# Second-half weights at set times, one store for each quad, and squares one step sooner in a fused attention and gated-MLP kernel

## The chip, the cores and the metric

The kernel runs on one core of one Trainium2 chip. The metric is the device time of that core in microseconds (us). A profile is one execution of the program under the hardware profiler. Its span is about 1.8 us shorter than the time of the same execution. The engines are called TensorE (PE in the profile), VectorE (DVE), ScalarE (ACT), GpSimd (POOL) and SyncE (SP, which issues the DMAs; SPq is its queue).

## The reference, cut to what matters

```python
def reference(A_x, A_wqkv, A_wo, B_x, B_w_in, B_w_sp, B_b_sp, B_w_out, gate_w):
    def _A_ref(x, wqkv, wo):          # S = 2048, D = 1024, H = 32 heads of 32
        ...                           # each position sees 8 keys at distances 0, 2, ..., 14
        logits = jnp.einsum('bhsd,bhswd->bhsw', q, kg) * scale
        attn = _softmax(logits, axis=-1)
        o = jnp.einsum('bhsw,bhswd->bhsd', attn, vg)
        return o.transpose(0, 2, 1, 3).reshape(B, S, D) @ wo

    def _B_ref(x, w_in, w_sp, b_sp, w_out):          # Fh = 1792
        z = _gelu(jnp.einsum('bsd,df->bsf', x, w_in))
        z1 = z[..., :Fh]
        z2 = _layernorm(z[..., Fh:], axis=-1)
        g = jnp.einsum('ts,bsf->btf', w_sp, z2) + b_sp[None, :, None]
        return jnp.einsum('bsf,fd->bsd', z1 * g, w_out)

    g = _sigmoid((x * gate_w).sum(-1, keepdims=True))
    return g * _A_ref(...) + (1 - g) * _B_ref(...)
```

## The kernel before

The kernel runs in stages: the projections of attention, then z2 (two halves of its columns, p = 0 with 7 quads and p = 1 with 8), then z1 (7 steps of two quads), then the spatial product with w_sp, then the two output products. Attention's own arithmetic is done by VectorE and runs alongside the projections and z2.

Every large product is done in "quads": a Strassen-like scheme with 7 products of half-size blocks on four PSUM banks. Two quads run interleaved as a pair, which is 56 matmuls: about 10.5 us for z2 (448 columns each) and 12 us for z1 (512 columns). Between the products of a quad come additions that VectorE makes from one PSUM bank into another (`plus`). TensorE cannot go on without them: the fifth product overwrites the bank Y that the first addition reads. What stands in VectorE's queue in front of such an addition can therefore stop TensorE.

```python
    def chain(A11, A12, A22, S1, S2, S3, S4, B11, ..., vs, put, share, N, ...):
        def plus(out, a):
            dve(N / 960.0 + 0.14, clock["PE"] + 0.2)
            last_add[0] = nc.vector.tensor_tensor(out[:, n], a[:, n], vs, ALU.add)   # L485
            return last_add[0]
        ...
        product(X, pairs(A11, B11), True, N)             # 1; product() is L424
        last_seed[0] = nc.scalar.copy(Y[:, n], X[:, n])
        yield
        product(V, pairs(S1, T1), True, N)               # 2
        with tc.high_priority():
            share(vs, V[:, n])                           # L503
        yield
        product(Y, pairs(S2, T2), False, N)              # 3
        with tc.high_priority():
            plus(Z, Y)                                   # first addition
        yield
        product(X, pairs(A12, B21), False, N)            # 4
        ...
        yield
        product(Y, pairs(S3, T3), False, N)              # 5
        ...
            inst = plus(V, Y)                            # second addition
        ...
        product(Z, pairs(S4, B22), False, N)             # 6
        ...
        product(W, pairs(A22, T4), False, N)             # 7
```

The weights of a quad also need four sums on VectorE (`sums4`, S1 to S4) before its second product. For p = 1 these are four sums of 128 x 1792, about 1.08 us each, and for each z1 step four sums of 0.42 us.

The order of instructions in the z2 stage is fixed while the program is built. A builder keeps a virtual clock for each engine (`clock`), collects loads (`due`) and small pieces of VectorE work (`fill`) with the time at which each may start, and puts an instruction into the program when the virtual clock comes to that time (`advance`). `act`, `dve` and `pe` book time on it. `settle` then pins the order on every engine. From z1 on, the framework's scheduler decides the order by itself.

```python
    def load_later(p, at, gap):           # z2 weights: 8 steps of 2 DMAs
        def landed(t):
            land[0] += 1
            if land[0] == KT:
                fill.extend((t, 1.05, f) for f in wz_sums(p))
        for n, f in enumerate(load_wz(p)):
            dma(at + gap * n, 0.65, f, landed)
    ...
    load_later(1, clock["PE"], 1.2)
    mark(banks[4:8], ZC)
    for n in range(0, len(quads), 2):     # z2: attention's VectorE work is filled in by step()
        ...
        run(*[z2_quad(*q) for q in quads[n:n + 2]], step=quad_step)
    drain()                               # the rest of attention
    settle()
    live[0] = False
    ...                                   # z1
    for fp in range(3):
        load_w1(fp)                       # two DMAs each
    w1_sums(0)
    mark(banks, 512, ZC)                  # one matmul of 64 columns on each bank
    for fp in range(NFH):
        if fp + 1 < NFH:
            w1_sums(fp + 1)
        for a in ((), (0,), (1, 2), (3, 4), (5, 6), (7,), ())[fp]:
            load_raw(0, a)                # transposing load of w_sp, behind the last z1 store
        run(z1_quad(fp, 0), z1_quad(fp, 1), hooks={2: lambda: between(fp)})   # between: squares
        ...                               # normalize(n) when four more rows have their squares
        if fp + 3 < NFH:
            load_w1(fp + 3)
```

`load_raw` writes a part of SBUF in which attention's buffers stood, so the first of these loads also waits for the last store of attention's output to DRAM (o_d).

Of the kernel before, what the change touches and what calls it, by code (L numbers as in the profile page):

```python
# [13 lines left out]
P = 128  # L14
# [11 lines left out]
FH = 1792  # L26
# [32 lines left out]
def kernel(  # L59
# [31 lines left out]
    z1_d = dpool.tile([4, P, NF * 512], BF, name="z1_d")  # L91
# [161 lines left out]
    def dma(ready, dur, f, landed=None):  # L253
        if not live[0]:
            return f()
        item = [ready, dur, f, landed]
        due.append(item)
        return item

    def issue(item):  # L260
        if item in due:
            due.remove(item)
            ready, dur, f, landed = item
            sp = take("SP", 0.62, max(ready, lanes[-8]))
            end = take("DMA", 1.2 * dur, sp + 0.6) + 1.1
            lanes.append(end)
            f()
            if landed is not None:
                landed(end)
# [148 lines left out]
    last_store = [None]  # L418
    wait_for = [None, None, None]
# [385 lines left out]
    def z2_quad(p, i, side=None):  # L805
        vs = vz_slots[(i + p) % 2]
        w, s = wz[p], wzs[p]

        share = nc.vector.tensor_copy if p else nc.scalar.copy
        return chain([w[0][:, k, :] for k in K4], [w[0][:, 4 + k, :] for k in K4], [w[1][:, 4 + k, :] for k in K4],  # L810
                     *[[s[q][:, k, :] for k in K4] for q in range(4)], *x_tiles(i), vs,
                     lambda m, a, bank: z2_gelu(p, i, m, a, bank), share, ZC, flip=True, side=side, lean=LEAN[p])

# [8 lines left out]
    def square(n, x, junk):  # L822
        c = slice(x * HF, (x + 1) * HF)
        return nc.scalar.activation(junk[:, c], z2[:, z2_row(n), c], ACT.Square, accum_out=(s2, s2h)[x][:, n:n + 1])  # L824
# [46 lines left out]
    def load_later(p, at, gap):  # L871
        land = [0.0]

        def landed(t):
            land[0] += 1
            if land[0] == KT:
                fill.extend((t, 1.05, f) for f in wz_sums(p))
        for n, f in enumerate(load_wz(p)):
            dma(at + gap * n, 0.65, f, landed)
# [32 lines left out]
    load_later(1, clock["PE"], 1.2)  # L912
    mark(banks[4:8], ZC)
    junk = reg(R_OFF + 12288, FH)
    SQ_AT = (2, 9)
    for n in range(0, len(quads), 2):
        p, i = quads[n]
        if p == 1 or quads[n + 1][0] == 1:
            t = clock["PE"]
            while fill or due:  # L920
                t += 0.25
                advance(t)
        count = [0]

        def quad_step():
            hold[0] = count[0] != 1
            step()
            count[0] += 1
            if p == 1 and (NG - 2, 1) in multiplied and count[0] in SQ_AT and squares[0][0] < 2 * i and len(squares) > 32 - SQH:
                act(0.9, clock["PE"])  # L930
                square(*squares.pop(0), junk)
        run(*[z2_quad(*q) for q in quads[n:n + 2]], step=quad_step)
    hold[0] = False
    drain()
    settle()
    live[0] = False
    pinned.clear()
# [40 lines left out]
    def load_raw(c, a):  # L978
        row = 4 * c + (a % 4) + 8 * (a // 4)
        inst = sync.dma_start_transpose(raw_slots[c][:, :, a, :], wsp_v[row])  # L980
        tc.add_manual_dep(inst.ins, last_store[0].ins.name, NOSYNC, reason="behind the stores")
# [19 lines left out]
    w1_slots = [free(R_OFF + o, 2048).rearrange("p (k f c) -> p k f c", k=KT, f=2) for o in (36864, 30720, 32768)]  # L1001
    ws_slots = [free(R_OFF + o, 2048, F16).rearrange("p (q k c) -> p q k c", q=4, k=4) for o in (38912, 34816)]
    z1s_slots = [free(T1_OFF + 2048 * r, 2048).rearrange("p (f a t) -> p f a t", f=2, a=2) for r in range(2)]
    zv_slots = [free(R_OFF + 20480 + 1024 * r, 1024, F32) for r in range(2)]

    def load_w1(fp):
        for f in range(2):
            sync.dma_start(w1_slots[fp % 3][:, :, f, :], win_v[:, :, HF * f + fp * P:HF * f + (fp + 1) * P])
# [5 lines left out]
    def z1_quad(fp, c):  # L1014
# [6 lines left out]
        def gelu(f, a, bank):  # L1021
            last_gelu[0] = nc.scalar.activation(z1s[:, f, a, :], bank[:], ACT.Gelu_apprx_tanh)  # L1022

        def store():
            for a in range(2):
                dst = z1_d[c + 2 * a].rearrange("p (f t) -> p f t", f=NF)[:, fp:fp + NFH + 1:NFH, :]
                last_store[0] = sync.dma_start(dst, z1s[:, :, a, :])
# [9 lines left out]
    def between(fp):  # L1037
        left = max(6 - fp, 1)
        for _ in range(-(-len(squares) // left)):
            sq = square(*squares.pop(0), z1_junk)  # L1040
            tc.add_manual_dep(sq.ins, last_seed[0].ins.name, NOSYNC, reason="behind the first copies of the quads")

    for fp in range(3):
        load_w1(fp)
    w1_sums(0)
    mark(banks, 512, ZC)
    for fp in range(NFH):
        if fp + 1 < NFH:
            w1_sums(fp + 1)
        for a in ((), (0,), (1, 2), (3, 4), (5, 6), (7,), ())[fp]:  # L1050
            load_raw(0, a)
        if fp == 6:
            wsp_sums(0, 0)
        run(z1_quad(fp, 0), z1_quad(fp, 1), hooks={2: lambda: between(fp)})
        while fp and ready[0] + 4 <= (squares[0][0] if squares else 16):
            n = ready[0]
            nc.vector.tensor_tensor(s2[:, n:n + 4], s2h[:, n:n + 4], s2[:, n:n + 4], ALU.add)
            normalize(n)
# [4 lines left out]
    def load_z1(n):  # L1063
        c, fp = divmod(n, NFH)
        for a in range(2):
            src = z1_d[c + 2 * a].rearrange("p (f t) -> p f t", f=NF)[:, fp:fp + NFH + 1:NFH, :]
            sync.dma_start(z1_slots[n % 2][:, :, a, :], src)
# [211 lines left out]
```

## Time and profile before

| before | |
|---|---|
| times | 680.09, 680.32, 680.32 us: median 680.32 us |
| the profiled execution | 683.96 us (span 682.2 us, mean granted clock 0.995) |
| TensorE busy | 97% of the span |

TensorE is the bound nearly everywhere. The page's first part gives each engine's busy time, share of the span and number of instructions. The clock row gives the granted TensorE clock in tenths of full speed (9 is 90% or more) for 40 slices of about 17 us:

```profile
PE 662.7 (97%) x4193; PEld 317.2 (47%) x4193; DVE 453.6 (66%) x671; ACT 294.3 (43%) x619; POOL 6.3 (1%) x15
...
PEclk9999999999998999999999999999999999999999
```

So the question is what lies in the remaining holes. As a measure, I summed over all pairs of successive matmuls the time from start to start, less columns/2.4 GHz. In this document "holes" means that sum over a stretch, worked out from the trace. A matmul of 448 columns that waits for nothing starts 0.187 us after the one before. From 197 to 380 us, the stretch that the change touches, the profiled execution has 15.9 us of such excess. The waits view says on what (line of the waiter and of what it waited for; us in total, number, longest):

```profile
PE psum_all L424 <- DVE psum_all L485: 8.6, 5, 4.8
```

The timeline of TensorE in the first half of z2, which runs from about 197 to 240 us (start, duration, the group, and in brackets the idle time before it and what ended it) shows two of them:

```profile
205.04 10.75 PE L424 MATMUL psum_all<-arena 128*128 128x448 f16 x56 [1.45 <-DVE psum_all L485]
220.62 5.73 PE L424 MATMUL psum_all<-arena 128*128 128x448 f16 x18 [4.83 <-DVE psum_all L485]
```

The timeline of VectorE says what stood in front of the two additions (L485): first four sums of the first z1 weights, of which the first is shown (128 x 512, each 0.42 us), and later three sums of the second z2 weights (128 x 1792), which themselves had waited 3.03 us for their load. These weights are for the second half, from about 240 us on; their sums only stood in front of additions of the first.

```profile
202.90 0.42 DVE L560 TENSOR_TENSOR arena<-arena 128x512 f16<-128x512 bf16 x1
...
204.36 0.62 DVE L485 TENSOR_TENSOR psum_all<-psum_all,arena 128x448 f32<-128x448 f32 x1
...
216.81 3.22 DVE L556 TENSOR_TENSOR arena<-arena 128x1792 f16<-128x1792 bf16 x3 [3.03 <-DMA arena<-in_B_w_in_dram]
219.94 1.16 DVE L485 TENSOR_TENSOR psum_all<-psum_all,arena 128x448 f32<-128x448 f32 x2
```

After the long hole the clock is halved for a while. The windows view (stretch, length, then busy time and instructions of PE, of its weight loads, of DVE, ACT and POOL, then the clock, the share of the DMA engines and GB/s) shows 12 matmuls in 4.28 us, against 0.187 us each at full clock:

```profile
218.00:224.90 6.90, 4.28 (x12) 1.72 (x12) 5.77 (x7) 1.75 (x6) 0.00 (x0) 0.52 0.02 8
```

The Trainium skill ("TensorE: Matmul & The Clock Gate", Part 1) names two states of the clock for a kernel like this one, full and half, and says that an idle window of about 3.4 us halves it. This trace agrees: after 4.83 us of idleness the clock is 0.50 for 6.83 us.

SyncE's queue: all loads and stores of this stage are issued by this one queue, in order. The "arena<-in_B_w_in_dram" at 191.38 and 193.16 are the two loads of the first z1 weights, which the scheduler has placed here on its own, among attention's band stores (band_d). The 16 others are the second z2 weights. att_L is attention's load of its last logits.

```profile
191.38 0.42 SPq L186 DMA_DIRECT2D arena<-in_B_w_in_dram  x1
191.85 1.26 SPq L186 DMA_DIRECT2D band_d<-arena  x2
193.16 0.64 SPq L186 DMA_DIRECT2D arena<-in_B_w_in_dram  x1
193.95 4.68 SPq L186 DMA_DIRECT2D band_d<-arena  x2
198.68 1.50 SPq L186 DMA_DIRECT2D arena<-in_B_w_in_dram  x2
200.28 1.25 SPq L186 DMA_DIRECT2D band_d<-arena  x2
201.58 3.96 SPq L186 DMA_DIRECT2D arena<-in_B_w_in_dram  x6
205.64 1.57 SPq L186 DMA_DIRECT2D att_L<-band_d  x2
207.27 5.71 SPq L186 DMA_DIRECT2D arena<-in_B_w_in_dram  x8
```

The Trainium skill ("Perfetto Trace Analysis", DMA Instruction — HWDGE) says how such a line is to be read: it starts when the waits of the DMA have been met and ends when the sequencer is free for the next, and neither the wait before nor the movement of the data is in it. The trace agrees: the last of these loads was issued by 213.0 us and landed at 216.58 us.

In the z1 stage VectorE waits three times for w_in (2.51, 2.95 and 2.93 us), and TensorE loses about 0.4, 0.9 and 1.5 us behind that. VectorE's line for the last of them, and TensorE's:

```profile
344.16 0.43 DVE L560 TENSOR_TENSOR arena<-arena 128x512 f16<-128x512 bf16 x1 [2.93 <-DMA arena<-in_B_w_in_dram]
```

```profile
345.25 5.12 PE L424 MATMUL psum_all<-arena 128*128 128x512 f16 x23 [1.30 <-DVE psum_all L485]
```

At the end of z1 the first spatial product waits for sums (L560) that stand behind the last normalization (L951). VectorE's line and TensorE's:

```profile
373.40 2.71 DVE L951 TENSOR_SCALAR arena<-arena,mean,rstd 128x1792 f16<-128x1792 bf16 x4 [1.12 <-POOL rstd L948]
```

```profile
377.37 4.92 PE L424 MATMUL psum_all<-arena 128*128 128x512 f16 x22 [1.25 <-DVE arena L560]
```

### The profile page before, as it was taken

The numbers are of one execution on the slowest core, as the hardware profiler recorded it, in microseconds if no ns is written. First come the engines' busy times: TensorE is split into PE (matmuls) and PEld (weight loads), VectorE is DVE, ScalarE is ACT, GpSimd is POOL, SyncE is SP. The second block draws the span as 40 slices with busy tenths as digits, with TensorE's granted clock in tenths as the row PEclk, the third lists the DMA queues.
The fourth block names the chain that finished last, engine by engine and source line by source line (L and its number), as shares of the span: only waits on it lengthen the run. The fifth ranks groups of instructions, "written<-read, shape, count | busy, mean of one in ns | idle before, by whom it ended". The sixth has DMA issues, their size and how long they took to land.

```text
span 682.2 us, 10810 instructions
## 1 busy us (share of the span) xinstructions
PE 662.7 (97%) x4193; PEld 317.2 (47%) x4193; DVE 453.6 (66%) x671; ACT 294.3 (43%) x619; POOL 6.3 (1%) x15
## 2 busy tenths in 40 slices
PE   8999999999986999999999999999999999999997
PEld 4544466444443455444444444444444444444443
DVE  2520799948996899997569866788775694333301
ACT  3444666556586656687875221212212122222221
POOL 1000000000000000000000000000000000000000
PEclk9999999999998999999999999999999999999999
DMA  9978563987496021338994297648356299954100
GB/s 232 185 182 223 120 151 84 245 178 184 81 242 155 1 61 60 81 106 216 259 215 144 64 182 167 142 126 274 93 151 166 58 215 181 190 127 102 48 31 32
DMA packets 243301, 98.17 MB, mean 144 GB/s; under 512 B 190241, under 2 KB 236721, under 8 KB 243249
## 3 DMA queue, kind: packets, MB, share of 16 engines
q1 hardware_dynamic: 242560, 97.01, 59.3%
q8 instruction: 33, 0.54, 0.4%
q10 hardware_dynamic: 688, 0.46, 0.2%
q14 instruction: 20, 0.16, 0.1%
HBM read 45.10 MB, written 36.61 MB: 120 GB/s over the span
## 4 chain that ended last, share of the span: by engine, by line
PE 79%; DMA 6%; ACT 4%; DVE 4%; issue 4%; SPq 1%; POOL 0%; POOLq 0%; ACTq 0%; DVEq 0%
PE psum_all L424 63%; PE psum_all L282 11%; PE psum_all L292 3%; DMA arena<-in_B_w_in_dram 2%; ACT arena L352 2%; SPq L186 1%; PE psum_all L344 1%; DMA att_L<-band_d 1%; DMA band_d<-arena 1%; DMA arena<-v_d 1%; DVE psum_all L485 1%; PE psum_all L307 1%; ACT arena L794 1%; DVE arena L951 0%; DMA arena<-o_d 0%
## 5 line engine op out<-in xcount | busy, mean ns | idle before, releaser
L424 PE MATMUL psum_all<-arena 128*128 128x512 f16 (+5 forms) x2436 | 501.5, 368 | 10.4 <-DVE psum_all L485 8.6
L424 PEld LDWEIGHTS <-arena 128*128 128x128 f16 (+1 forms) x2436 | 238.4, 98 | 272.2 <-issue 14.8
L282 PE MATMUL psum_all<-arena 128*128 128x512 bf16 x512 | 114.8, 379 | 0.7 <-ACT gl_s L295 0.6
L282 PEld LDWEIGHTS <-arena 128*128 128x128 bf16 x512 | 48.4, 98 | 57.2 <-issue 1.3
L687 DVE TENSOR_TENSOR arena<-arena,att_A 128x2048 f16<-128x2048 bf16 (+1 forms) x44 | 73.5, 1704 | 0.3
L285 ACT CAST arena<-psum_all 128x512 bf16<-128x512 f32 x64 | 37.4, 586 | 51.5 <-PE psum_all L282 51.3
L560 DVE TENSOR_TENSOR arena<-arena 128x512 f16<-128x512 bf16 (+3 forms) x38 | 21.3, 573 | 53.3 <-PE psum_all L424 25.3
L442 ACT COPY psum_all<-psum_all 128x512 f32<-128x512 f32 (+1 forms) x30 | 15.8, 527 | 79.0 <-PE psum_all L424 78.3
L794 ACT ACTIVATE arena<-psum_all 128x448 bf16<-128x448 f32 x64 | 34.2, 546 | 23.6 <-PE psum_all L424 12.8
L485 DVE TENSOR_TENSOR psum_all<-psum_all,arena 128x448 f32<-128x448 f32 (+1 forms) x58 | 37.3, 659 | 7.3 <-ACT psum_all L519 3.7
L562 DVE TENSOR_TENSOR arena<-arena 128x512 f16<-128x512 bf16 (+3 forms) x38 | 21.5, 571 | 28.4 <-PE psum_all L424 15.8
L1022 ACT ACTIVATE arena<-psum_all 128x512 bf16<-128x512 f32 x56 | 30.6, 598 | 19.0 <-DVE psum_all L485 12.2
L691 DVE TENSOR_TENSOR arena<-arena 128x2048 f16<-128x2048 f16 (+1 forms) x22 | 37.2, 1703 | 0.1
L352 ACT CAST arena<-psum_all 128x1988 f16<-128x1988 f32 (+3 forms) x25 | 33.9, 1357 | 4.6 <-DMA band_d<-arena 2.0
L463 ACT COPY psum_all<-psum_all 128x512 f32<-128x512 f32 (+1 forms) x30 | 15.9, 528 | 45.8 <-PE psum_all L424 44.8
L453 ACT COPY psum_all<-psum_all 128x512 f32<-128x512 f32 (+1 forms) x30 | 15.8, 528 | 40.5 <-PE psum_all L424 39.9
L448 ACT COPY arena<-psum_all 128x512 f32<-128x512 f32 (+1 forms) x30 | 16.2, 544 | 37.4 <-PE psum_all L424 32.0
L824 ACT ACTIVATE arena<-arena 128x896 bf16<-128x896 bf16 x32 | 30.0, 943 | 0.0
L561 DVE TENSOR_TENSOR arena<-arena 128x512 f16<-128x512 f16 (+3 forms) x38 | 21.4, 571 | 7.6 <-PE psum_all L424 7.5
L1202 DVE TENSOR_TENSOR arena<-psum_all,arena 128x512 bf16<-128x512 f32 x8 | 5.5, 690 | 29.0 <-ACT psum_all L463 29.0
L292 PE MATMUL psum_all<-arena 128*128 128x385 bf16 x128 | 22.6, 327 | 0.3 <-DVE arena L315 0.3
L563 DVE TENSOR_TENSOR arena<-arena 128x512 f16<-128x512 bf16 (+3 forms) x38 | 21.2, 569 | 1.7 <-PE psum_all L424 1.6
(90 smaller groups left out, 394.2 us busy)
## 6 DMA issues: line engine op xcount, KB each, us to landing
arena<-v_d SPq DMA_DIRECT2D x8, 960.0 KB, 6.0
z_d<-arena SPq DMA_DIRECT2D x28, 256.0 KB, 2.8
arena<-z_d SPq DMA_DIRECT2D x28, 256.0 KB, 3.6
zg_d<-arena SPq DMA_DIRECT2D x56, 128.0 KB, 2.3
arena<-zg_d SPq DMA_DIRECT2D x32, 224.0 KB, 3.3
band_d<-arena SPq DMA_DIRECT2D x28, 248.5 KB, 5.1
arena<-in_A_wqkv_dram SPq DMA_DIRECT2D x16, 256.0 KB, 4.3
o_d<-arena SPq DMA_DIRECT2D x4, 1024.0 KB
```

What stands on the lines that cost most here:

```text
L282: nc.tensor.matmul(ps[:], w[:, t, kt, :], xT[:, kt, 512 * c:512 * (c + 1)], start=(kt == 0), stop=(kt == KT - 1))
L285: nc.scalar.copy(dst[:, :, 256 * c:256 * (c + 1)], ps[:].rearrange("p (n e) -> p e n", e=2))
L292: nc.tensor.matmul(ps[:, 0:VP + 1], xT[:, kt, i * P:(i + 1) * P], wvp[:, kt, :], start=(kt == 0), stop=(kt == KT - 1))
L352: nc.scalar.copy(dst, src)
L424: nc.tensor.matmul(bank[:, 0:N], lhsT, rhs, start=(start and m == 0), stop=(m == n - 1), skip_group_check=True)
L485: last_add[0] = nc.vector.tensor_tensor(out[:, n], a[:, n], vs, ALU.add)
L562: nc.vector.tensor_tensor(s_out[2], a11, a21, ALU.subtract)
L687: lambda ws=ws, in0=in0, in1=in1: tt(p5[:, ws], in0[:, ws], in1[:, ws], ALU.mult)), False
L691: lambda a=p3[:, ws], b=p3[:, ws.start + 4:ws.stop + 4]: tt(a, a, b, ALU.add)), not n
L794: nc.scalar.activation(z2[:, i + 8 * a, ZC * c:ZC * (c + 1)], bank[:, 0:ZC], ACT.Gelu_apprx_tanh, accum_out=s1[:, 4 * n + c:4 * n + c + 1])
L824: return nc.scalar.activation(junk[:, c], z2[:, z2_row(n), c], ACT.Square, accum_out=(s2, s2h)[x][:, n:n + 1])
L1022: last_gelu[0] = nc.scalar.activation(z1s[:, f, a, :], bank[:], ACT.Gelu_apprx_tanh)
```

## The change

Its intent is to take these four holes away:

1. The second z2 weights load at set times: they start 3 us later on the builder's clock and one step every 2.0 us, not 1.2, and a semaphore keeps each from being issued before the ScalarE instruction at that place. Their sums come 0.5 us later on that clock (`LATE`). (The semaphore and `LATE` hold for the first half's weights too.)
2. The first z1 weights load at a set place, before the fourth quad of the second half, and their sums are filled in from there.
3. The copies `share` of the second half move from VectorE to ScalarE, and attention's tail runs on into the first z1 pair (`drain` after it).
4. z1 goes to DRAM in one store for each quad (14 of 512 KB, not 28 of 256 KB), and comes back in as many loads. In the same stage each transposing load of w_sp is now put behind the latest z1 weights as well as behind the last z1 store, and only the first of a pair is asked for before the quads (`raws`).
5. The squares for the layernorm end one z1 step (a pair of quads) sooner, and the last normalization has high priority, so that it comes ahead of the spatial product's sums.

```diff
-    z1_d = dpool.tile([4, P, NF * 512], BF, name="z1_d")
+    z1_d = dpool.tile([2, P, NF * 1024], BF, name="z1_d")
 ...
     def issue(item):
 ...
+            if timed:
+                settle()
+                behind, at = pinned[gate_act.ins.engine], len(nc.cur_bb.bb.instructions)
             f()
+            if timed:
+                for i in nc.cur_bb.bb.instructions[at:]:
+                    tc.add_manual_dep(i, behind, SYNC, reason="not sooner")
 ...
-        share = nc.vector.tensor_copy if p else nc.scalar.copy
+        share = nc.scalar.copy
 ...
-                fill.extend((t, 1.05, f) for f in wz_sums(p))
+                fill.extend((t + LATE, 1.05, f) for f in wz_sums(p))
         for n, f in enumerate(load_wz(p)):
-            dma(at + gap * n, 0.65, f, landed)
+            dma(at + gap * n, 0.65, f, landed, True)
 ...
-    load_later(1, clock["PE"], 1.2)
+    load_later(1, clock["PE"] + 3.0, 2.0)
 ...
+        if p == 1 and i == 3:
+            dma(clock["PE"], 2.9, lambda: load_w1(0), w1_landed(0))
 ...
         run(*[z2_quad(*q) for q in quads[n:n + 2]], step=quad_step)
     hold[0] = False
-    drain()
-    settle()
-    live[0] = False
-    pinned.clear()
+    while fill or any(x[3] is not None for x in due):
+        advance(max(clock["PE"], clock["DVE"]) + 0.5)
 ...
         def store():
-            for a in range(2):
-                dst = z1_d[c + 2 * a].rearrange("p (f t) -> p f t", f=NF)[:, fp:fp + NFH + 1:NFH, :]
-                last_store[0] = sync.dma_start(dst, z1s[:, :, a, :])
+            dst = z1_d[c].rearrange("p (f t) -> p f t", f=NF)[:, fp:fp + NFH + 1:NFH, :]
+            last_store[0] = sync.dma_start(dst, z1s.rearrange("p f a t -> p f (a t)"))
 ...
     def between(fp):
-        left = max(6 - fp, 1)
+        left = max(5 - fp, 1)
 ...
-    for fp in range(3):
-        load_w1(fp)
-    w1_sums(0)
     mark(banks, 512, ZC)
+    for fp in (1, 2):
+        dma(clock["PE"] + 1.0, 2.9, lambda fp=fp: load_w1(fp), w1_landed(1) if fp == 1 else None)
     for fp in range(NFH):
 ...
-        run(z1_quad(fp, 0), z1_quad(fp, 1), hooks={2: lambda: between(fp)})
+        run(z1_quad(fp, 0), z1_quad(fp, 1), hooks={2: lambda: between(fp), 4: lambda: [load_raw(0, a) for a in raws[1:]]},
+            step=None if fp else step)
+        if fp == 0:
+            drain()
+            settle()
+            live[0] = False
+            pinned.clear()
 ...
-            normalize(n)
+            with tc.high_priority() if n == 12 else nullcontext():
+                normalize(n)
```

## The prediction

> **What bounds the kernel now.** TensorE. The page gives PE 97% of a 682.2 us span. Start-to-start times of its matmuls exceed columns/2.4 GHz by only about 15 us in total. After 197 us it sits in a few holes (timeline view):
>
> - 203.2: 1.6 us. PE waits for a DVE addition (L485) that stands behind four z1 weight sums (202.90 to 204.44).
> - 215.4: 4.8 us. DVE stands 3.03 us for the second z2 weights (DMA arena<-in_B_w_in), then makes three sums (3.22 us) before the two additions that PE needs.
> - 220.6 to 225.0: the granted clock is 0.50 for 6.83 us from 218.2; 12 matmuls start 0.37 us apart, not 0.187: 2.2 us lost. The Trainium skill ("TensorE: Matmul & The Clock Gate", Part 1) has the clock halve after about 3.4 us of idleness; this trace agrees, after 4.8 us.
> - 320, 333, 343.6: 0.4, 0.9, 1.5 us. DVE stands 2.5, 2.95, 2.93 us for z1 weights, whose second half is issued behind four z1 stores and lands 4.5 to 5.0 us later.
> - 375: 1.7 us. The first spatial quad's sums stand behind the last normalization (371.5 to 376.1).
> - 278 to 287: about 0.5; 543: about 0.5.
>
> Together about 14 us; the floor this way is about 666.
>
> **What the change does.** PE's work is the same (same rows in the built order). On DVE, the z1 sums leave 202.9; the second z2 sums move behind the second pair's additions and three to five attention products; the 16 copies of the second half's quads (0.6 us each, 10 us) move to ACT, so attention ends about 10 us sooner. ACT then has about 8 us of work in each 10.5 us pair: room enough. Paced z2 weights (SP needs about 0.65 us for each DMA, 16 of them) let the band stores and the last logits' load go first. z1 stores fall from 28 to 14, of double length: about 1.3 us less of SP per pair before the weights behind them. The last normalization moves one pair ahead.
>
> **On the critical path.** 203: 1.4 gained. 215 with its slow clock: 4.8 + 2.2, less about 1.0 for additions that still come late (a maximum that waits for logits stands before one, products before two). z1 waits: the loads come 1.3 to 2 us sooner, DVE still stands about 1, PE hardly: 2.2 of 2.8. 375: 1.5. New losses where attention's tail meets the first z1 pair: 0.8. Sum: 1.4 + 6.0 + 2.2 + 1.5 - 0.8 = 10.3 us.
>
> **Prediction: 670.0 us** (1.5% faster), 8 times in 10 between 667.0 and 676.0. Faster by over 2%: 0.05; within 2%: 0.94; slower by over 2%: 0.01.
>
> **What would show it.** Clock 1.00 throughout 200 to 280 (windows view), no PE gap over 3 us; no DVE wait over 1 us on arena<-in_B_w_in near 216; at 310 to 345 such waits under 1.5 us and no PE gap over 0.5; no PE gap at about 365 before the spatial quads; DVE about 10 us less and ACT about 10 more between 230 and 280.
>
> **What would make it wrong.** The set times are the builder's own clock: if the chip lags it, the z2 sums or the last logits' maxima still stand in front of PE's additions, and a stall over 3 us brings the slow clock back (4 to 7 us of the gain). A z1 sum ahead of its load in the first z1 pair would do the same.

## The result, and the profile after

| | before | after |
|---|---|---|
| median of all runs of that job | 680.32 us (4 runs, 680.09 to 681.06) | 673.11 us (4 runs, 672.68 to 675.22) |
| ratio | | 0.9898, 95% interval 0.9876 to 0.992 |
| profiled execution | 683.96 us (span 682.2) | 675.22 us (span 673.4) |

A ratio here is the mean time of one kernel's fast runs over that of the other's of the same rounds, so it is not quite the ratio of the medians quoted. The gain is 7.2 us by the medians, where 10.3 us were predicted; the time lies inside the predicted range, 3.1 us above its centre.

The holes of the two profiled executions, by stretch of the span, with a second profiled execution of the changed kernel from a later job beside them:

| holes, us | 197–240 (z2) | 240–270 (z2) | 270–300 (z2 to z1) | 300–345 (z1) | 345–380 (z1 to spatial) |
|---|---|---|---|---|---|
| before | 9.2 | 0.4 | 0.9 | 3.3 | 2.1 |
| after | 4.2 | 0.6 | 1.9 | 0.8 | 0.7 |
| after, second profile | 3.3 | 0.6 | 1.9 | 0.8 | 0.7 |

The spans of the first two differ by 8.8 us. Their holes in these five stretches fall from 15.9 to 8.2 us, and the sum over the whole span by 8.6 us: the holes tell nearly the whole difference of these two executions. The medians differ by only 7.2 us, because the profiled execution of before was 3.6 us slower than that kernel's median, and that of after 2.1 us slower than its own. I come back to this.

The page, and the wait of TensorE for the additions in the waits view:

```profile
PE 661.3 (98%) x4193; PEld 316.9 (47%) x4193; DVE 449.8 (67%) x663; ACT 296.8 (44%) x627; POOL 6.9 (1%) x15
...
PEclk9999999999999999999999999999999999999999
```

```profile
PE psum_all L431 <- DVE psum_all L492: 1.2, 3, 0.5
PE psum_all L576 <- ACT arena L801: 0.8, 1, 0.8
```

The slow clock is gone, its waits for the additions fell from 8.6 to 1.2 us, and one new wait has come (L576, at the marks). VectorE's timeline: the z1 sums no longer stand in front of the addition (now L492) at 202.23; a maximum of attention (L657) waits 1.94 us in front of another (before, it waited 1.42 us behind the additions); and the z2 sums come without a wait, behind the additions.

```profile
202.23 0.63 DVE L492 TENSOR_TENSOR psum_all<-psum_all,arena 128x448 f32<-128x448 f32 x1
...
207.30 0.29 DVE L657 TENSOR_TENSOR att_m<-att_L 128x256 f16<-128x256 f16 x1 [1.94 <-DMA att_L<-band_d]
...
220.94 4.21 DVE L563 TENSOR_TENSOR arena<-arena 128x1792 f16<-128x1792 bf16 x4
...
226.21 1.16 DVE L492 TENSOR_TENSOR psum_all<-psum_all,arena 128x448 f32<-128x448 f32 x2
```

TensorE's timeline shows that small holes remain before these additions, and the one at the marks:

```profile
214.94 3.94 PE L431 MATMUL psum_all<-arena 128*128 128x448 f16 x20 [0.36 <-DVE psum_all L492]
...
226.89 11.07 PE L431 MATMUL psum_all<-arena 128*128 128x448 f16 x56 [0.55 <-DVE psum_all L492]
...
281.64 0.36 PE L576 MATMUL psum_all<-arena 128*128 128x64 bf16 x7 [0.77 <-ACT arena L801]
```

SyncE's queue: the band stores now go first and without a load among them, and the timed z2 weights follow. Two of these still stand ahead of the last logits (att_L), which is what the maximum waited for.

```profile
191.17 6.03 SPq L186 DMA_DIRECT2D band_d<-arena  x6
200.91 0.80 SPq L186 DMA_DIRECT2D arena<-in_B_w_in_dram  x2
201.89 1.27 SPq L186 DMA_DIRECT2D att_L<-band_d  x2
203.22 7.99 SPq L186 DMA_DIRECT2D arena<-in_B_w_in_dram  x8
```

In z1 the waits for w_in shrink; the longest on VectorE is this one, and TensorE hardly notices it (0.8 us of holes in the whole stretch). At the end of z1 there is no hole: TensorE's line runs through the start of the spatial product, which comes at about 365 us.

```profile
338.48 0.42 DVE L567 TENSOR_TENSOR arena<-arena 128x512 f16<-128x512 bf16 x1 [1.53 <-DMA arena<-in_B_w_in_dram]
```

```profile
354.63 17.69 PE L431 MATMUL psum_all<-arena 128*128 128x512 bf16 x80
```

### The profile page after: what moved, and what is told of

It reads as the page before. It is cut to its first block, busy times and chain, and to the rows that moved or that the text cites. A ratio compares the mean times of both kernels' runs of the same rounds, so it can differ in the third digit from the quotient of the medians.

```text
span 673.4 us, 10760 instructions
## 1 busy us (share of the span) xinstructions
PE 661.3 (98%) x4193; PEld 316.9 (47%) x4193; DVE 449.8 (67%) x663; ACT 296.8 (44%) x627; POOL 6.9 (1%) x15
## 4 chain that ended last, share of the span: by engine, by line
PE 86%; ACT 5%; DVE 5%; DMA 2%; issue 1%; SPq 0%; POOL 0%; ACTq 0%; DVEq 0%
PE psum_all L431 67%; PE psum_all L288 14%; PE psum_all L298 3%; ACT arena L358 2%; PE psum_all L350 1%; DVE psum_all L492 1%; ACT arena L801 1%; DMA band_d<-arena 1%; DVE arena L977 1%; DMA att_L<-band_d 1%; DVE arena L698 1%; PE psum_all L313 1%; DMA arena<-o_d 0%; PE psum_all L576 0%; ACT arena L291 0%
## 5 line engine op out<-in xcount | busy, mean ns | idle before, releaser
L567 DVE TENSOR_TENSOR arena<-arena 128x1024 f16<-128x1024 f16 (+3 forms) x36 | 20.6, 582 | 47.6 <-PE psum_all L431 26.7
L492 DVE TENSOR_TENSOR psum_all<-psum_all,arena 128x448 f32<-128x448 f32 (+1 forms) x58 | 37.2, 660 | 9.1 <-PE psum_all L431 5.2
L569 DVE TENSOR_TENSOR arena<-arena 128x1024 f16<-128x1024 f16 (+3 forms) x36 | 20.6, 580 | 29.3 <-PE psum_all L431 12.5
L470 ACT COPY psum_all<-psum_all 128x512 f32<-128x512 f32 (+1 forms) x30 | 15.9, 529 | 46.2 <-PE psum_all L431 45.1
L568 DVE TENSOR_TENSOR arena<-arena 128x1024 f16<-128x1024 f16 (+3 forms) x36 | 20.6, 582 | 8.2 <-PE psum_all L431 7.9
L657 DVE TENSOR_TENSOR att_m<-att_L 128x256 f16<-128x256 f16 x8 | 2.3, 288 | 29.4 <-DMA att_L<-band_d 29.3
```

Of the source, the lines that this page charges most:

```text
L567: first = nc.vector.tensor_tensor(s_out[0], a21, a22, ALU.add)
```

## The experiments

Twelve kernels ran in three jobs, each on one chip with its own runs of the kernel before: in the first job its median was 682.17 us, in the second 683.21 us, in the third 679.67 us. All were correct against the reference. Times of different jobs are only compared by their ratios to before. In the traces of the first job some matmul records are missing from about 282 us on, and each missing one counts as a false hole of 0.22 us; so for that job only the stretch 197–240 is compared.

My theory after the first result was this. The z2 part of the gain comes from the pacing, the medians gain less than the profile because the slow clock costs less than its matmuls lose, and the z1 part comes from the fewer stores. The rivals are in the expectations.

### Pacing undone

The changed kernel with the second z2 weights at once again, as before, and without the wait; the rest of the change stays.

```diff
-                fill.extend((t + LATE, 1.05, f) for f in wz_sums(p))
+                fill.extend((t + (0.0 if p else LATE), 1.05, f) for f in wz_sums(p))
-            dma(at + gap * n, 0.65, f, landed, True)
+            dma(at + gap * n, 0.65, f, landed, not p)
-    load_later(1, clock["PE"] + 3.0, 2.0)
+    load_later(1, clock["PE"], 1.2)
```

> The changed kernel with the second z2 weights loaded as before (at once, 1.2 us apart by the builder's clock, no wait on ScalarE, no margin before the sums); all other parts of the change kept. Theory 'place of the sums': the four sums again stand ahead of the additions that TensorE needs, VectorE waits 2 us or more for DMA arena<-in_B_w_in near 215, PE has a gap of 3 to 5 us, the granted clock drops to 0.5 for some microseconds: 677 to 681 us. Rival 'the other parts made the gain' (copies moved to ScalarE, z1 sums gone from 203): VectorE reaches the sums after the weights have landed, no gap over 1 us, 672 to 674.5 us.

Measured: 676.97 us (4 runs, 676.02 to 678.61), ratio 0.9933 (0.991 to 0.9956). VectorE does wait for the weights again, but less, and TensorE's hole is half of the one before; the clock stays at 1.00. VectorE's line, then TensorE's:

```profile
211.41 3.22 DVE L563 TENSOR_TENSOR arena<-arena 128x1792 f16<-128x1792 bf16 x3 [1.89 <-DMA arena<-in_B_w_in_dram]
```

```profile
215.22 3.94 PE L431 MATMUL psum_all<-arena 128*128 128x448 f16 x20 [2.23 <-DVE psum_all L492]
```

The last weights landed at 211.2 us, with the same issue times asked for as in the kernel before, where they landed at 216.6. So something other than the pacing had made them late there. Neither expectation is met: the hole of 2.23 us lies between the theory's 3 to 5 us and the rival's 1 us. What the pacing itself is worth follows from the next run of the same job.

### The order without the wait

Only the semaphore wait "not sooner" goes; the order of instructions on every engine is that of the changed kernel.

```diff
-            dma(at + gap * n, 0.65, f, landed, True)
+            dma(at + gap * n, 0.65, f, landed, not p)
```

> The changed kernel without the semaphore wait that keeps each part of the second z2 weights from being issued sooner than its set time; the order of instructions on every engine is the same. Theory 'the order decides': the loads are issued at most a few us sooner, nothing is crowded, 672.5 to 674 us, PE's gaps between 200 and 240 as in the changed kernel within 0.5 us. Rival 'the set times decide' (loads issued early crowd the logits' and v loads out): VectorE's waits for att_L and for v grow by 1 us or more and the time by 1.5 us or more, to 674.8 or above.

Measured: 674.34 us (4 runs, 673.96 to 674.84), ratio 0.9887 (0.9868 to 0.9905), holes in 197–240 of 3.25 us. That is not worse than the changed kernel. The maximum's wait for att_L is gone (1.94 and 1.01 us in the two profiles of the changed kernel), as the loads no longer hold the queue. So the order and the places that the builder fixes are what works, and the wait adds nothing. The Trainium skill ("DMA: Bandwidth & Descriptors", Anatomy of one DMA — SWDGE (gpsimd) path, in a note on DMA engines in general) says that a DMA's semaphore wait happens on the sequencer that issues it, before dispatch. The traces agree: in the changed kernel the queue stood from 197.20 to 200.91 us before the first timed load, and att_L followed at 201.89; here it went at 200.05. Against "pacing undone" this run is 2.6 us better by the medians and 2.0 by the spans: the worth of the pacing (with `LATE`) once the rest of the change is there.

### TensorE kept busy in the hole of the kernel before

To measure the cost of the slow clock alone, the kernel before got 84 matmuls of 64 columns, into unused columns of a bank, at the place of the long hole.

```diff
+        def filler():
+            for _ in range(84):
+                nc.tensor.matmul(last_v[0][:, ZC:512], xT[:, 4, 0:P], xT[:, 4, 0:512 - ZC], start=False, stop=True, ...)
-        run(*[z2_quad(*q) for q in quads[n:n + 2]], step=quad_step)
+        run(*[z2_quad(*q) for q in quads[n:n + 2]], step=quad_step, hooks={5: filler} if n == 2 else {})
```

> The kernel before with 84 small matmuls (128x64, into columns that nobody reads) put where TensorE stands for 4.8 us at 215; nothing else changed. Theory 'the slow clock costs 2.2 us of its own': with TensorE active in the hole the granted clock stays 1.0, the matmuls after it start 0.19 us apart, and the time is 1.5 to 2.3 us less, 678.0 to 678.8. Rival 'VectorE, 95% busy, would have held TensorE back anyway': the clock stays up but the gaps come back within the next 15 us, less than 0.7 us gained, 679.6 to 680.5. If the fillers do not count as activity the clock drops as before and the run tells nothing.

Measured: 681.4 us (6 runs, 680.17 to 683.39), ratio 0.9991 (0.9972 to 1.0011). TensorE's timeline, with the fillers in the first line:

```profile
215.55 2.61 PE L937 MATMUL psum_all<-arena 128*128 128x64 bf16 x84
219.79 3.94 PE L425 MATMUL psum_all<-arena 128*128 128x448 f16 x20 [1.62 <-DVE psum_all L486]
224.09 7.05 PE L425 MATMUL psum_all<-arena 128*128 128x448 bf16 x36 [0.36 <-ACT psum_all L521]
```

The clock was 0.999 or 1.0 in five of the six runs (0.997 in the slowest, 683.39 us), and in the trace the matmuls after the hole start 0.19 us apart. But small stalls come in behind them (0.52, 0.32, 0.25 and 0.31 us), which the slow matmuls had hidden. The holes of 197–240 fall from 9.2 to 5.4 us plus the 2.2 us that the fillers themselves stream: 1.6 us, not the 2.2 us that I had counted. Of these 1.6 us, 0.65 lie in the hole itself, which is shorter because the weights landed at 215.75 us and not at 216.58, though the fillers change nothing before it. What followed the hole fell by only 0.9 us (0.6 with the stall of 0.31 us, which comes after 240). In the time the gain is 0.6 us with an interval of 1.3 either way, so the time decides nothing. The traces of "pacing undone" and of the z1 loads moved (below), in which the clock stayed up too, show stalls of 0.52 and 0.25 us at the same two copies of ScalarE.

### The sums alone moved, in the kernel before

The theory held that removing the stall at 203 would only lengthen the one at 215, since the weights land when they land. In the kernel before, only the four sums of the first z1 weights were put off until the fourth quad of the second half.

```diff
-    w1_sums(0)
+    with tc.high_priority():
+        for f in sums4_steps([ws_slots[0][:, q] for q in range(4)], ...):
+            tc.add_manual_dep(f().ins, mid_add.ins.name, NOSYNC, reason="not sooner")
```

> The kernel before with only the four z1 weight sums taken from 203 us to behind the additions of the second half of z2. The prediction added 1.4 us for this. Theory 'hidden behind the weights': the gap at 203 goes, but VectorE then only waits longer for the weights at 215 and the gap there grows by as much: 680.0 to 680.7 us. Rival 'additive': 678.6 to 679.2 us.

Measured: 681.79 us (6 runs, 679.32 to 684.27), ratio 0.9996 (0.9974 to 1.0019). In the trace the stall at 203 is gone and the later one did not grow, but shrank: TensorE idles 3.93 us (4.83 before), and the clock is halved for 3.41 us (6.83 before). The weights landed by 214.3 us. SyncE's line for the last eight, VectorE's, then TensorE's:

```profile
207.22 4.76 SPq L186 DMA_DIRECT2D arena<-in_B_w_in_dram  x8
```

```profile
214.31 3.22 DVE L556 TENSOR_TENSOR arena<-arena 128x1792 f16<-128x1792 bf16 x3 [1.48 <-DMA arena<-in_B_w_in_dram]
```

```profile
218.13 22.09 PE L424 MATMUL psum_all<-arena 128*128 128x448 f16 x107 [3.93 <-DVE psum_all L485]
```

The holes of 197–240 went from 9.2 to 6.4 us. But this doesn't refute the theory. The weights landed 2.5 us sooner than in the profile of before, although the last eight began to be issued at the same time (207.22 and 207.27 us); in the filler run, with the same queue, they landed at 215.75. So the landing differs from one execution to the next. The hole still ends with the three sums behind the weights: had these come at the time of before, it would have been some 6.4 us by this trace (3.93 + 2.5, an estimate), as the theory says. The time shows no gain (0.3 us, with 1.5 either way). This step is inconclusive.

### Two stores again

The changed kernel with the z1 stores and loads halved again, as before.

```diff
-            dst = z1_d[c].rearrange("p (f t) -> p f t", f=NF)[:, fp:fp + NFH + 1:NFH, :]
-            last_store[0] = sync.dma_start(dst, z1s.rearrange("p f a t -> p f (a t)"))
+            for a in range(2):
+                dst = z1_d[c + 2 * a].rearrange("p (f t) -> p f t", f=NF)[:, fp:fp + NFH + 1:NFH, :]
+                last_store[0] = sync.dma_start(dst, z1s[:, :, a, :])
```

> The changed kernel with z1 written to and read from DRAM in two transfers per quad, as before. The prediction put 2.2 us on the loads of the z1 weights coming sooner behind fewer stores. Theory 'the stores delay the weights': between 300 and 345 VectorE again waits 2 us or more for DMA arena<-in_B_w_in at the sums of the quads, TensorE's holes there add up to 1.5 to 3 us, the time is 674.5 to 676 us (ratio to before 0.991 to 0.994). Rival 'the order of loads and transposes alone made it' : waits under 1 us, holes under 0.7 us, the time as the changed kernel.

Measured: 676.37 us (4 runs, 674.64 to 677.96), ratio 0.9898 (0.9871 to 0.9926), the very ratio of the changed kernel's first job. The waits of VectorE for w_in in z1 are 0.3 us each, and the holes of 300–345 are 1.3 us, against 0.8 with one store and 3.3 before. The waits and the time are as the rival forecast; the holes lie between the two forecasts. The fewer stores are worth about half a microsecond there in these traces, and my reason for the z1 gain falls.

### The squares one step later

```diff
-        left = max(5 - fp, 1)
+        left = max(6 - fp, 1)
-            with tc.high_priority() if n == 12 else nullcontext():
-                normalize(n)
+            normalize(n)
```

> The changed kernel with the squares spread over six z1 pairs again and the last normalization at its ordinary priority. Theory 'the last normalization stood in front of the spatial sums': a hole of 1.4 to 1.7 us returns at the start of the spatial stage (about 364 us), released by VectorE, and nothing else changes: ratio to before 0.991 to 0.9935. Rival 'the extra VectorE room would have taken the normalization in time anyway': hole under 0.5 us, time as the changed kernel.

Measured: 676.89 us (4 runs, 676.69 to 677.64), ratio 0.9908 (0.9884 to 0.9933). The hole returns where it was expected, with the normalization in front of it, and the holes of 345–380 are 2.1 us again, as before. TensorE's line at it came back with the same idle time as in the kernel before, 1.25 us. VectorE:

```profile
367.38 2.72 DVE L977 TENSOR_SCALAR arena<-arena,mean,rstd 128x1792 f16<-128x1792 bf16 x4 [1.12 <-POOL rstd L974]
```

This step of the prediction (1.5 us) is confirmed in the trace at 1.4 us. The difference in ratio from other runs of that job is of that size, but within the intervals.

### The first z1 weights early again, with the pacing

```diff
+    dma(clock["PE"], 2.9, lambda: load_w1(0), w1_landed(0))
     load_later(1, clock["PE"] + 3.0, 2.0)
 ...
-        if p == 1 and i == 3:
-            dma(clock["PE"], 2.9, lambda: load_w1(0), w1_landed(0))
```

> The changed kernel with the first z1 weights loaded (512 KB, two issues) and summed at the start of the z2 quads, as before, and nothing else undone. Theory 'they crowd the stretch at 200': the logits' load and the z2 weights come 1.3 us later or more, VectorE's waits for att_L or for the weights grow by 1 us or more, TensorE's holes between 200 and 240 grow from 4.2 us (sum over 10 us slices) to 5.5 us or more. Rival 'paced weights leave room': holes within 0.7 us of the changed kernel's.

Measured: 674.13 us (4 runs, 673.74 to 674.83), ratio 0.9867 (0.9843 to 0.9892), the best of its job, with holes of 2.6 us in 197–240. The theory that the two loads crowd the z2 weights wherever they stand early is refuted. They stand behind four of the six band stores here, and the z2 weights are paced.

### Marks inside z2, and attention put off

A trial for a better kernel. The marks (64-column matmuls that make the banks' last columns valid) go inside the last z2 quads, the wait goes as above, and attention's work is put off further in favour of the additions (`FR` weighs how far a piece of attention may reach past an addition's time).

```diff
-    FR, LATE = 0.4, 0.5
+    FR, LATE = [0.4], 0.5              # and FR[0] = 0.8 from the z2 quads on
 ...
         product(X, pairs(A11, B11), True, N)
+        if marks:
+            mark([X], 512, ZC)
 ...
         product(V, pairs(S1, T1), True, N)
+        if marks:
+            mark([V], 512, ZC)
 ...
-    mark(banks, 512, ZC)
```

> An attempt at a better version of the changed kernel: no wait that holds the second z2 weights to their set time; the marks of the accumulators' last columns made inside the last z2 quads, not all at the end; and from the z2 quads on, the builder puts an attention product ahead of a quad's addition only where 80% of it fits before the addition is due (40% before). Theory: the two holes near 209 (0.9 us, behind the maximum that waits for the logits) go, the hole at the marks (0.9 us) goes, the holes behind products at 214, 226 and 238 (1.6 us together) shrink to a third: 2.5 to 3 us less than the changed kernel, ratio to before 0.985 to 0.9875. Rival: attention's products, put off, pile up before the z1 quads and open new holes there of the same size: ratio 0.988 to 0.991.

Measured: 676.52 us (6 runs, 675.3 to 676.76), ratio 0.9896 (0.9874 to 0.9918): no gain, as the rival forecast. The z2 holes did shrink (2.0 us in 197–240, 0.9 in 270–300), but those of 300–345 grew to 4.8 us. SyncE's queue shows what went with it, and VectorE's timeline what came of that:

```profile
309.91 0.54 SPq L186 DMA_DIRECT2D o_d<-arena  x1
...
315.75 7.48 SPq L191 DMA_TRANSPOSE arena<-in_B_w_sp_dram  x3
```

```profile
329.82 0.43 DVE L571 TENSOR_TENSOR arena<-arena 128x512 f16<-128x512 bf16 x1 [3.70 <-DMA arena<-in_B_w_in_dram]
```

Attention's output was stored at 309.9 us, not 298.5. The first transposing load starts at 315.75, when that store had landed (315.69); three of them then hold the queue for 7.5 us, and the next z1 weights, issued at 324.63, stand behind them. The kernel before looks alike (store at 310.85, three transposing loads from 316.69 on). This suggested a new theory for z1: it is the end of attention that sets the z1 holes, and the copies moved to ScalarE bring it forward.

### The copies on VectorE again

```diff
-        share = nc.scalar.copy
+        share = nc.vector.tensor_copy if p else nc.scalar.copy
```

> The changed kernel with the 16 copies of the second half's z2 quads on VectorE again. The loads of the spatial weights write where attention's output stood, so the first of them waits until o_d has been stored. New theory 'attention's end sets the z1 stage': with 10 us more on VectorE, o_d goes at 308 to 311 us and not at 298.5, three of the transposed loads are issued in one row behind it, two z1 weight loads come late, VectorE waits 2 us or more for DMA arena<-in_B_w_in twice, and TensorE's holes between 300 and 345 grow from 0.8 us to 2.5 to 4.5 us; time 2 to 4 us above the changed kernel in the same job. Old theory (the prediction's: fewer stores did it): holes there under 1.2 us.

Measured: 674.4 us (4 runs, 674.09 to 675.86), ratio 0.9925 (0.9904 to 0.9946), against 0.9908 for the changed kernel in the same job. The queue shows what the new theory expects: a late store of attention's output (at 306.59 us), then three transposing loads in a row.

```profile
313.49 6.64 SPq L191 DMA_TRANSPOSE arena<-in_B_w_sp_dram  x3
```

VectorE waits 1.03 and 2.08 us for w_in, but the holes of 300–345 are only 1.1 us. The time is 1.1 us above the changed kernel, not 2 to 4. The new theory has the chain of events right and the size wrong. Counted from the first matmul of z1, attention's output is stored at 26.1 us here, at 24.6 in the kernel before and at 16.6 in the changed one. So attention ends even later than before, and a late end alone doesn't give the 3.3 us of the kernel before.

### The first z1 loads alone moved, in the kernel before

The last open question of the z2 stage was why the weights landed at 216.6 us before and at 211.2 us in "pacing undone". In the kernel before, both the sums (as above) and the two loads of the first z1 weights were put off; nothing else was changed.

```diff
+            inst = sync.dma_start(w1_slots[fp % 3][:, :, f, :], ...)
+            if fp == 0:
+                tc.add_manual_dep(inst.ins, early_add.ins.name, SYNC, reason="not sooner")
```

> The kernel before with the first z1 weights' two loads (512 KB) taken out from among the band stores to behind the second z2 weights, besides their sums moved later (as in the run with the sums alone). Theory 'their place in the queue delays the z2 weights': the last z2 weights land at 211 to 213 us (before: 216.6)[...] and the clock stays at 1.0; holes from 197 to 240 sum to 3.5 to 5 us (before 9.2; sums alone 6.4); 677 to 679 us by the first job's scale, ratio 0.992 to 0.996. Rival 'pacing the z2 weights is what mattered': landing after 214[...], the slow clock returns.

Measured: 676.86 us (4 runs, 676.12 to 678.21), ratio 0.9958 (0.9934 to 0.9983). SyncE's queue without the two loads:

```profile
190.83 3.83 SPq L186 DMA_DIRECT2D band_d<-arena  x4
...
203.53 5.88 SPq L186 DMA_DIRECT2D arena<-in_B_w_in_dram  x8
```

TensorE's line at the hole that was 4.83 us:

```profile
215.17 3.94 PE L424 MATMUL psum_all<-arena 128*128 128x448 f16 x20 [1.40 <-DVE psum_all L485]
```

The last eight weights are issued from 203.53 us on, not 207.27, and the last landed at 211.18 us. In this profile the clock never drops (one of the four runs had 0.997), and the holes of 197–240 fall from 9.2 to 3.75 us, with no pacing at all. The sums were moved too, but with the sums alone the last eight were still issued from 207.22 us on, and the clock dropped. So two loads of 256 KB, which nobody needed for another 80 us, were the main cause of the late issue; that this kept the hole short enough for the full clock rests on one profile of each kernel. The two loads take only 0.42 and 0.64 us in the queue. Of the 3.7 us, 0.55 were there already in front of the first of them, and most of the rest lies in the band stores among them, which took longer to issue (7.19 us for six before; here 5.08). Why they did is not shown.

### The changed kernel with both, and the changed kernel once more

A last version takes the early z1 weights (above) and the marks inside z2, without the other edits of the failed trial; the loads keep their order. The changed kernel, unchanged, ran beside it.

```diff
+    dma(clock["PE"], 2.9, lambda: load_w1(0), w1_landed(0))
     load_later(1, clock["PE"] + 3.0, 2.0)
 ...
+        if marks:
+            mark([X], 512, ZC, False)     # after the 1st product; [V] after the 2nd
 ...
-    mark(banks, 512, ZC)
+    for _ in banks:
+        pe((512 - ZC) / 2400.0)           # only the builder's clock
```

> The version to beat both: the changed kernel, its first z1 weights loaded and summed early again (which ran at 0.9867 of before), and the marks of the accumulators' last columns made inside the last z2 quads. Theory: the hole of 0.9 us at the marks goes and nothing else moves (the load order is the same): holes from 270 to 300 under 1.2 us, 0.8 to 1.2 us less than with early weights alone; ratio to before 0.984 to 0.9865, and 1.5 to 3.5 us under the changed kernel run in this job. Rival: the wait only moves to the first z1 quads: no gain over early weights alone.

> The changed kernel as it is, on the same chip as the two above, to compare within one job: ratio to before 0.988 to 0.991; holes as in its first profile within 0.7 us in each stretch.

Measured: 671.93 us (4 runs, 671.86 to 672.38), ratio 0.9886 (0.9867 to 0.9905), against 673.26 us (6 runs, 672.86 to 675.35), ratio 0.9908 (0.989 to 0.9926), for the changed kernel. The slowest run of the new version is faster than the fastest of the changed kernel, and by the medians it is 1.3 us (0.2%) better; by the ratios the intervals overlap. Over early weights alone (0.9867, in another job) no gain is shown. The hole at the marks is gone: between the last quads TensorE waits 0.21 us at most.

```profile
274.39 25.88 PE L431 MATMUL psum_all<-arena 128*128 128x448 f16 x120 [0.21 <-ACT psum_all L506]
```

### The holes of all runs

| holes, us | 197–240 | 240–270 | 270–300 | 300–345 | 345–380 | ratio |
|---|---|---|---|---|---|---|
| before | 9.2 | 0.4 | 0.9 | 3.3 | 2.1 | 1 |
| sums moved, in before | 6.4 | | | | | 0.9996 |
| fillers, in before | 5.4 (+ 2.2) | | | | | 0.9991 |
| z1 loads and sums moved, in before | 3.75 | 0.4 | 0.85 | 2.7 | 2.1 | 0.9958 |
| pacing undone | 4.7 | | | | | 0.9933 |
| copies on VectorE | 3.1 | 0.4 | 2.45 | 1.1 | 0.7 | 0.9925 |
| changed kernel | 4.2 / 3.3 | 0.6 | 1.9 | 0.8 | 0.7 | 0.9898 / 0.9908 |
| squares later | 4.35 | 0.6 | 1.9 | 0.8 | 2.1 | 0.9908 |
| two stores | 3.8 | 0.6 | 1.9 | 1.3 | 0.7 | 0.9898 |
| marks inside, attention off | 2.0 | 0.4 | 0.9 | 4.8 | 0.7 | 0.9896 |
| no wait | 3.25 | | | | | 0.9887 |
| early z1 weights | 2.6 | 0.4 | 2.1 | 0.8 | 0.7 | 0.9867 |
| early z1 weights, marks inside | 2.4 | 0.4 | 1.1 | 0.8 | 0.7 | 0.9886 |

## Why the prediction was right or wrong

The time and the class were right, but the centre was 3.1 us too low, and two of the four reasons (the pacing, the fewer stores) were not the ones that the runs show, or only a part of them.

**The bound and the list of holes** were right. TensorE's holes account for 8.6 of the 8.8 us between the two profiled executions.

**"203: 1.4 gained."** That stall is gone, in the changed kernel and where only the sums were moved. That it is worth 1.4 us by itself is not shown: alone it brought nothing in the time (0.9996), and the later hole can take it up.

**"4.8 + 2.2, less about 1.0"** for the stall at 215 and the slow clock. This is the term that was mis-sized. For the z2 stage, with the 1.4 above, 7.4 us were predicted; the holes fell by 5.0 us in the first profile and 5.9 us in the second. What stays is larger than the 1.0 us that I allowed: additions behind attention's products (0.5, 0.7 and 0.5 us), a copy behind a table load of ScalarE (0.6 us), and the maximum's wait. The filler run adds that the slow clock's 2.2 us are not all to be had: with the clock up, other stalls came out and only 0.6 to 0.9 us were left.

**What the sum was taken from** is the second part of that miss. I summed the holes of one profiled execution of before, and that execution took 683.96 us where the median was 680.32. The runs of before show why such a number isn't safe: they differ by up to 4.7 us within a job, and in the third job its 11 executions fall into 5 with a mean granted clock of 0.999 or 1.0, which average 678.9 us, and 6 with 0.995 to 0.997, which average 680.7. (In the other two jobs the difference goes the same way, 0.7 and 1.0 us, with only two and one runs on the one side.) All four runs of the changed kernel had 0.999 or 1.0. So before meets the slow clock in most of its executions, more or less of it, and the profile showed one with much of it (0.995). That the clock makes these runs slow is a correlation; the one run that kept the clock up, with fillers, didn't decide it. The chip is a rival: the record doesn't say on which one that profile was taken, and the medians of before in the three jobs, each on its own chip, reach from 679.67 to 683.21 us. Nor does the clock explain the changed kernel's own profile, 2.1 us over its median at 1.0.

**"Paced z2 weights let the band stores and the last logits' load go first."** The order was right but for two weights ahead of the logits; the pacing as the cause was only a part. Two loads of z1 weights among the band stores, of which I had costed the sums alone, were what made the z2 weights late in the queue. Moving these and their sums in the kernel before, with no pacing, brings 5.4 of the 9.2 us of holes and the full clock in the profile, and 2.8 us of the time (0.9958 x 680 us; by the interval 1.2 to 4.5). Pacing with the loads early again, behind four of the band stores, works as well (holes of 2.6 us). Once the loads are out, the pacing brings 2 to 2.6 us more. Pacing alone in the kernel before was not run, so how the gain divides between the two is not known. The semaphore wait that belongs to the pacing adds nothing.

**"z1 waits: 2.2 of 2.8."** The size was right (holes 3.3 to 0.8 us), the reason was not; the right size is luck as far as these runs show. With two stores again the holes are 1.3 us. With the copies back on VectorE and a late end of attention they are 1.1 us; with an end still later (30.6 us after z1's start, among other edits) they are 4.8 us. So the gain is covered by more than one part of the change, and each of those that I took away alone was made up for. How it divides among the loads' places, the new places of the transposing loads (which no run undid), attention's end and the place of the sums between the additions stays open.

**"375: 1.5."** Right: 1.4 us, and the hole returns when only that part is undone.

**"Where attention's tail meets the first z1 pair: 0.8"** lost. Right in size (the stretch 270–300 went from 0.9 to 1.9 us), wrong in place. The loss is at the marks: one of these waits 0.77 us for ScalarE's gelu to have read its bank. It went when the marks were moved inside the quads.

**"The 16 copies of the second half's quads (0.6 us each, 10 us)"** was a slip. The view of that line, which I had not opened, shows 8 of them on VectorE (number, then shortest, median and longest in ns), so 5 us; in the changed kernel all 15 are on ScalarE. Before, then after:

```profile
L503 DVE COPY arena<-psum_all x8: 615/618/624, 242.6 to 282.3; 128x448 f32<-128x448 f32 x8
```

```profile
L510 ACT COPY arena<-psum_all x15: 513/545/589, 200.8 to 276.5; 128x448 f32<-128x448 f32 x15
```

The expectation of the run that put the copies back repeats it. The slip cost little: attention's output still went out 12.4 us sooner (310.85 to 298.49 us). Of these, 4.4 us are only that z1 itself starts sooner. Counted from z1's start the output comes 8.0 us sooner (24.6 to 16.6 us), and with the copies back all of that is gone (26.1). Why 8 copies of 0.6 us are worth so much is not shown.

**Signs.** Of those named, these came true: clock 1.00 throughout, no hole over 3 us, no wait of VectorE for w_in near 216 us, and none at 365 us. One was missed by a little: a wait in z1 was 1.53 us, where "under 1.5" was named. One failed: between 230 and 280 us VectorE was to be busy about 10 us less and ScalarE about 10 us more. The windows view has 47.06 us before and 47.50 after for VectorE, and 29.88 and 36.67 for ScalarE.

## What to carry to other kernels

When a load lands late, look at everything that the same in-order queue issued before it, not only at the load's own time: here two loads that nobody needed for another 80 us, placed by a scheduler, went with a critical one being issued 3.7 us late. Before summing the holes of a profile, compare the time of the profiled execution with the median, on the same chip, and see whether the clock was lower in it; a hole that only some executions have is worth only its share. And where two repairs cover one fault, undoing one can show too little: do each alone in the kernel before as well. A single trace in which a hole shrank is not yet an effect of the edit; look first whether the load that ends the hole came at the same time.

## What the Trainium skill lacked or had wrong

- "TensorE: Matmul & The Clock Gate", Part 1, fits what the runs show: idle times of 1.40 and 2.23 us left the clock at 1.00, and 3.93 and 4.83 us halved it, for 3.41 and 6.83 us. It lacks that the loss isn't simply the sum over the slowed matmuls where another engine is nearly as busy: with the clock kept up, stalls of 0.52, 0.32, 0.25 and 0.31 us came out that the slow matmuls had hidden, and what followed the hole shrank by 0.6 to 0.9 us, not 2.2.
- The same page lacks that small matmuls in a gap are enough: 84 matmuls of 64 columns (2.6 us in all, in a wait of 4.2 us) went with a clock of 0.999 or 1.0 in five runs of six, against two of eleven of the kernel before in the same job.
- The same page has nothing on a stall in mid-kernel that slows the clock in some executions of one kernel and not in others: 11 runs of the kernel before on one chip had mean clocks of 0.995 to 1.0 and times of 678.44 to 682.26 us. The repaired kernel's ten had 0.999 or 1.0. That the clock made the times differ is a correlation.
- "Trainium Kernel Development and Optimization", Key Constraints, says that issuing DMAs from several engines only saves the sequencer's issue time. It has no size for that time, and here it matters. In the trace of the kernel before, a plain load or store (L186) held the queue for 0.55 us in the median, with a range of 0.33 to 5.05, and the seven transposing loads between 300 and 345 us for 1.7 to 4.1 us each, all in one in-order queue, where 16 loads of weights alone make some 11 us.
